# An early 64-byte store of zeros to every partition's rows of the output, in a streaming multiply-add

## The chip, the cores and the metric

The kernel runs on one core of one Trainium2 chip. The metric is the device time of one execution in microseconds (us), and the medians below are over repeated runs. Every profile shows the clock at 1.0.

## The reference, cut to what matters

```python
B, S, D = 1024, 16, 512          # x, y: bfloat16 (B, S, D); gamma: bfloat16 (D)
def reference(x, y, gamma):
    return x + gamma * y
```

Two inputs of 16.8 MB are read and one output of 16.8 MB is written, and there is little arithmetic.

## The kernel before

The 16384 rows of 512 elements are spread over 128 partitions, 128 rows (128 KB) each. They are handled in four pieces of 32 rows, so a piece is 32 KB a partition and 4 MB in all. The x loads go through the SyncE queue and the y loads through the ScalarE queue. The stores are issued behind all the loads of their queue.

```python
    nc.gpsimd.dma_start(out=gamma_row[:], in_=gamma.unsqueeze(0))
    nc.vector.memset(ones_row[:], 1.0)
    gamma_ps = psum_pool.tile([P, D], mybir.dt.float32)
    nc.tensor.matmul(gamma_ps[:], ones_row[:], gamma_row[:], start=True, stop=True)
    nc.vector.tensor_copy(out=gamma_sb[:], in_=gamma_ps[:])
    io_pool = ctx.enter_context(tc.tile_pool(name="io", bufs=SLOTS))     # SLOTS = 6
    # ... cut ...
    for c in range(n_pieces):                                            # PIECE = 32, four pieces
        r = slice(c * PIECE, (c + 1) * PIECE)
        # ... cut: xt, yt from io_pool ...
        nc.sync.dma_start(out=xt[:], in_=xv[:, r, :])
        nc.scalar.dma_start(out=yt[:], in_=yv[:, r, :])
        # ... cut: yt = yt * gamma_sb, then yt = xt + yt, both on VectorE ...
    for c in range(n_pieces):
        r = slice(c * PIECE, (c + 1) * PIECE)
        eng = nc.sync if c % 2 == 0 else nc.scalar
        eng.dma_start(out=ov[:, r, :], in_=ys[c][:])
```

## Time and profile before

| What | Before |
|---|---|
| time, median of 3 runs | 123.46 us (123.09 to 123.53) |
| span in the profile | 121.5 us |
| bytes moved | 50.33 MB, mean 414 GB/s |
| VectorE busy | 70.4 us (58%) |
| one multiply or one add of a piece | 8.7 us |

Lines of the page of the kernel before. They are the busy time of an engine, the two DMA rows in 40 slices of the span (busy share in tenths, then GB/s), the packet count, the DMA queues with packets, MB and share of the 16 engines' time, and the chain of work that ended last.

```profile
span 121.5 us, 80 instructions
PE 0.6 (0%) x1; PEld 0.1 (0%) x1; DVE 70.4 (58%) x10; POOL 0.8 (1%) x5
...
DMA  5899999999999999999999999989898989898992
GB/s 173 378 486 389 475 399 464 399 464 421 442 432 432 410 453 410 453 399 464 410 453 410 453 410 453 345 345 518 356 507 356 507 356 507 367 496 389 475 410 108
DMA packets 1760, 50.33 MB, mean 414 GB/s; under 512 B 224, under 2 KB 224, under 8 KB 224
...
q10 hardware_dynamic: 864, 25.17, 48.7%
q1 hardware_dynamic: 864, 25.17, 48.6%
q0 software_dynamic: 32, 0.00, 0.0%
...
DMA yt<-in_y_dram 53%; DVE yt L58 14%; DVE yt L64 14%; ACTq L57 0%
```

The DMA row is at 8 or 9 nearly everywhere while VectorE is busy little more than half the time, so the 16 DMA engines set the time. The Trainium skill (HBM Reference, Specifications (TRN2)) says that a core streaming alone measures about 425 GB/s, bounded by its 16 DMA engines. This trace agrees, with 414 GB/s over the whole span, start and end included. The chain names VectorE for 29% of the span (two lines of 14.3%), but meanwhile the DMA engines are busy with other transfers, so this share is no limit.

The trace also holds a record of every DMA packet (queue, start, duration, size). One packet here is one partition's 32 KB. Undisturbed it takes 1.213 us, and each engine has 96 of them: 96 x 1.213 = 116.4 us. From the first packet (1.76 us) to the last completion (119.95 us) are 118.2 us, so little is lost. There are two losses that all engines share. The first x packets take about 1.8 us. The y packets that start at 77.6 us take 1.79 to 2.13 us, which loses 0.75 us an engine. The second loss, two packets before the first result packet, is called **the stall** below. A view by windows shows it without the records (columns: window, its length, busy time of each engine, clock, DMA busy share, GB/s). The kernel before:

```profile
core 0: us, PE busy (x) PEld busy (x) DVE busy (x) POOL busy (x), PEclk, DMA share, GB/s
75.20:77.60 2.40, 0.00 (x0) 0.00 (x0) 2.40 (x1) 0.00 (x0) 1.00 1.01 437
77.60:79.54 1.94, 0.00 (x0) 0.00 (x0) 1.42 (x1) 0.00 (x0) 1.00 1.01 270
79.54:83.20 3.66, 0.00 (x0) 0.00 (x0) 0.35 (x1) 0.00 (x0) 1.00 1.02 439
```

In the third line the DMA share is still 1.01 but the rate is 270 GB/s instead of 437. A DMA engine counts as busy while a packet is on it, moving or not. (A packet is put into the window where it starts, so windows have to be cut at packet starts for such a reading.)

### The profile page before, as it was taken

To read this page: it belongs to the slowest core of one execution; us is meant where nothing else is said; L and a number is where in the kernel's file an instruction comes from. 1 tells how busy PE (TensorE), PEld (TensorE's weight loads), DVE (VectorE), ACT (ScalarE), POOL (GpSimd) and SP (SyncE) were. 2 spreads that over 40 slices of the span, in tenths; PEclk is the share of its full clock that TensorE was granted. 3 is DMA by queue.
4 is the path that set the end of the run, shared out by engine and by line. 5 is a ranking of instruction groups with operands and counts; after the bars stand their busy time and mean duration, and the time that the engine had idled before them with its cause. 6 is when DMAs were issued, how large, how long until landed. Compare 5 with 4: busy or idle time off the path is not lost.

```text
span 121.5 us, 80 instructions
## 1 busy us (share of the span) xinstructions
PE 0.6 (0%) x1; PEld 0.1 (0%) x1; DVE 70.4 (58%) x10; POOL 0.8 (1%) x5
## 2 busy tenths in 40 slices
PE   0001000000000000000000000000000000000000
PEld 0000000000000000000000000000000000000000
DVE  0002000499999399999679999907999990000000
POOL 2000000000000000000000000000000000000000
DMA  5899999999999999999999999989898989898992
GB/s 173 378 486 389 475 399 464 399 464 421 442 432 432 410 453 410 453 399 464 410 453 410 453 410 453 345 345 518 356 507 356 507 356 507 367 496 389 475 410 108
DMA packets 1760, 50.33 MB, mean 414 GB/s; under 512 B 224, under 2 KB 224, under 8 KB 224
## 3 DMA queue, kind: packets, MB, share of 16 engines
q10 hardware_dynamic: 864, 25.17, 48.7%
q1 hardware_dynamic: 864, 25.17, 48.6%
q0 software_dynamic: 32, 0.00, 0.0%
HBM read 33.56 MB, written 16.78 MB: 414 GB/s over the span
## 4 chain that ended last, share of the span: by engine, by line
DMA 53%; DVE 29%; ACTq 0%; issue 0%
DMA yt<-in_y_dram 53%; DVE yt L58 14%; DVE yt L64 14%; ACTq L57 0%
## 5 line engine op out<-in xcount | busy, mean ns | idle before, releaser
L58 DVE TENSOR_TENSOR yt<-yt,gamma_sb 128x16384 bf16<-128x16384 bf16 x4 | 34.8, 8692 | 18.9 <-DMA yt<-in_y_dram 18.9
L64 DVE TENSOR_TENSOR yt<-xt,yt 128x16384 bf16<-128x16384 bf16 x4 | 34.8, 8692 | 0.1
L47 DVE CAST gamma_sb<-gamma_ps 128x512 bf16<-128x512 f32 x1 | 0.7, 692 | 10.1 <-PE gamma_ps L46 10.1
L44 DVE MEMSET ones_row<- 1x128 bf16 x1 | 0.2, 165 | 0.8 <-PEq L85 0.8
L46 PE MATMUL gamma_ps<-gamma_row,ones_row 1*128 1x512 bf16 x1 | 0.6, 579 | 10.4 <-DMA gamma_row<-in_gamma_dram 10.4
L43 POOL DMA_DIRECT2D gamma_row<-in_gamma_dram x1 | 0.6, 607 | 0.8 <-POOLq L85 0.8
L46 PEld LDWEIGHTS <-ones_row 1*128 1x128 bf16 x1 | 0.1, 98 | 1.0 <-DVE ones_row L44 1.0
L85 POOL MEMSET const-bfloat16-1.0<- 128x1 bf16 x1 | 0.1, 97 | 0.0
L85 POOL MEMSET const-float32-0.0<- 128x1 f32 x1 | 0.1, 93 | 0.2 <-issue 0.2
L85 POOL MEMSET const-float32-1.0<- 128x1 f32 x1 | 0.1, 94 | 0.0
L85 POOL MEMSET const-uint8-127<- 128x1 uint8 x1 | 0.1, 94 | 0.0
## 6 DMA issues: line engine op xcount, KB each, us to landing
yt<-in_y_dram ACTq DMA_DIRECT2D x4, 4096.0 KB, 32.1
xt<-in_x_dram SPq DMA_DIRECT2D x4, 4096.0 KB, 40.5
out_dram<-yt SPq DMA_DIRECT2D x2, 4096.0 KB, 49.0
out_dram<-yt ACTq DMA_DIRECT2D x2, 4096.0 KB, 31.1
gamma_row<-in_gamma_dram POOLq DMA_DIRECT2D x1, 1.0 KB, 9.2
```

Of the source, the lines that this page charges most:

```text
L43: nc.gpsimd.dma_start(out=gamma_row[:], in_=gamma.unsqueeze(0))
L44: nc.vector.memset(ones_row[:], 1.0)
L46: nc.tensor.matmul(gamma_ps[:], ones_row[:], gamma_row[:], start=True, stop=True)
L47: nc.vector.tensor_copy(out=gamma_sb[:], in_=gamma_ps[:])
L58: nc.vector.tensor_tensor(out=yt[:], in0=yt[:], in1=gamma_sb[:, None, :].to_broadcast([P, PIECE, D]), op=mybir.AluOpType.mult,)
L64: nc.vector.tensor_tensor(out=yt[:], in0=xt[:], in1=yt[:], op=mybir.AluOpType.add)
L85: nc = _bacc.Bacc("TRN2", target_bir_lowering=False, num_devices=1)
```

## The change

Its intent is to store something to the output early, so that whatever the first write to it may cost is met before the first store of results. 64 bytes of zeros go to the start of every partition's rows through the GpSimd queue. The first store of results writes the same bytes, so it has to come after it and overwrites it.

```diff
     nc.vector.tensor_copy(out=gamma_sb[:], in_=gamma_ps[:])
+    prime_sb = const_pool.tile([P, 32], dt)
+    nc.vector.memset(prime_sb[:], 0.0)
+    nc.gpsimd.dma_start(out=ov[:, 0, 0:32], in_=prime_sb[:])
     io_pool = ctx.enter_context(tc.tile_pool(name="io", bufs=SLOTS))
```

## The prediction

> **What bounds the kernel now.** The DMA engines. The page's slice rows show DMA nine tenths busy or more nearly throughout, and 414 GB/s over the 121.5 us span; VectorE is busy 58%, the other engines almost never. The chain of waits (53% DMA, 29% VectorE) says it less directly, as queued transfers hide its VectorE part. In the packet records of the trace each of the 16 engines moves 96 data packets of 32 KB, at 1.213 us each when undisturbed: 116.4 us. The first packet starts at 1.8 us and the last completion is at 119.9 us: 118.2 us, so only 1.8 us is lost. Two losses hit all engines together: the first x packets take 1.82 us (0.6 us lost), and the y packets that start at 77.6 us take 1.8 to 2.1 us (mean 1.96; 0.75 us lost). The second comes two packets before the first result packet: queues run first in, first out, so the first store, issued at 40.6 us, moves only after all of x has landed, at 80.8 us. The other stores start without such a loss.
>
> **What the change adds.** One VectorE memset of 128x32 (the 1x128 one took 0.17 us; VectorE idles until 22.8 us) and a small DMA through GpSimd: 128 pieces of 64 bytes, eight an engine, behind the gamma load, whose packets were seen at 7.2 us and completions at 9.6 us. Small packets of that queue take turns with the two big queues, two packets of 1.213 us between turns: the pieces should move from about 9 us, and if each takes its own turn the last lands at about 32 us. The first store then waits for this DMA too (same bytes), but it can't move before 79 us, so that wait is free. The Trainium skill (DMA: Bandwidth & Descriptors, Specifications) says that below 512 bytes the engine does a read-modify-write; no run here shows that yet. Gamma's 64-byte packets took 0.011 us each. I estimate 0.01 to 0.1 us a piece, 0.1 to 0.8 us an engine, all of it on the critical path.
>
> **What it may remove.** The 0.75 us loss, if it is a cost of the first write to the output (something set up once for these addresses, that lasts 70 us). The small store then meets it early: either it is hidden there, because 64 bytes hold up little, and 0.75 us is gained; or it blocks load packets just as long, and nothing is gained. If the loss comes of turning from loads to stores, it stays, and the small store adds one or more of its own. Loads, multiplies, adds and stores keep their order on every engine.
>
> **Prediction.** 123.46 - half of 0.75 + about 0.2 = 123.2 us, range 122.3 to 124.3. Faster by over 2% (under 121.0): 0.02, since 1.8 us is all that is lost anywhere. Within 2%: 0.95. Slower by over 2%: 0.03, if every piece stalls its engine by 0.75 us (8 x 0.75 = 6 us).
>
> **What would show it.** Packet records: y packets near 77 us at 1.21 us mean the first-write theory holds; still 1.9 us, that it falls. Long load packets at 9 to 32 us show a loss that only moved. The slice rows stay as they are; packets rise by 144 (128 pieces, 16 completions); the first result store shows no wait for the small store.
>
> **What would make it wrong.** Stalls at every piece; a GpSimd queue that holds up the engines; the small store landing after 79 us.

## The result, and the profile after

The changed kernel takes 123.45 us (median of 4 runs, 123.19 to 123.60) beside 123.41 us before (4 runs). The ratio is 1.0005, with a 95% interval of 0.998 to 1.003: the same. Here and below a ratio is the mean time of one kernel's runs over that of the other's in the same rounds, so not quite the ratio of the medians.

The page of the changed kernel, the lines that answer to those above, then the new store's lines among the groups of instructions (busy us, mean ns, idle before) and the DMA issues (KB each, us from issue to landing):

```profile
span 121.6 us, 83 instructions
PE 0.6 (0%) x1; PEld 0.1 (0%) x1; DVE 70.4 (58%) x11; POOL 1.4 (1%) x6
...
DMA  6898989999999989898989898999899999999991
GB/s 172 366 496 367 498 388 474 399 463 420 442 453 409 474 388 485 377 485 377 485 377 485 377 496 366 345 388 474 388 474 399 463 399 463 409 453 442 420 463 54
DMA packets 1792, 50.34 MB, mean 414 GB/s; under 512 B 240, under 2 KB 256, under 8 KB 256
...
q0 software_dynamic: 64, 0.01, 0.0%
...
L52 POOL DMA_DIRECT2D out_dram<-prime_sb x1 | 0.6, 559 | 0.0
...
out_dram<-prime_sb POOLq DMA_DIRECT2D x1, 8.0 KB, 13.3
```

What SyncE's DMA queue waited for in the changed kernel (us in total, times, longest). The line of the loads is L61 here, that of the result stores L75:

```profile
SPq L75 <- DVE yt L69: 37.0, 1, 37.0
...
SPq L75 <- DMA xt<-in_x_dram: 0.9, 1, 0.9
```

The windows around the stall, changed kernel:

```profile
75.10:77.49 2.39, 0.00 (x0) 0.00 (x0) 2.39 (x1) 0.00 (x0) 1.00 0.98 411
77.49:79.54 2.05, 0.00 (x0) 0.00 (x0) 1.45 (x1) 0.00 (x0) 1.00 1.03 272
79.54:83.30 3.76, 0.00 (x0) 0.00 (x0) 0.00 (x0) 0.00 (x0) 1.00 1.02 436
```

There are three things to see here.

1. The small store cost next to nothing. It is 32 packets more (q0 from 32 to 64): 16 of data and 16 completions. The packet records show the data as one packet of 512 bytes an engine, at 12.0 to 12.4 us, of 0.027 us each; its completions come at 14.4 to 14.8 us. No load packet between 9 and 32 us took more than 1.213 us. No result store shows a wait for it: the waits of SyncE's queue name the add and an x load only.
2. The stall is still there. It moves 272 GB/s at a share of 1.03, and the 16 y packets at 77.5 to 78.5 us take 2.03 us in the mean, against 1.96 before.
3. So a term of gain that did not come and a cost that is too small to see leave the time where it was.

What remains is why the stall did not care.

### The profile page after: what moved, and what is told of

The parts are those of the page before. It is cut to its first block, busy times and chain, and to the rows that moved or that the text cites. A ratio compares the mean times of both kernels' runs of the same rounds, so it can differ in the third digit from the quotient of the medians.

```text
span 121.6 us, 83 instructions
## 1 busy us (share of the span) xinstructions
PE 0.6 (0%) x1; PEld 0.1 (0%) x1; DVE 70.4 (58%) x11; POOL 1.4 (1%) x6
## 4 chain that ended last, share of the span: by engine, by line
DMA 54%; DVE 29%; ACTq 0%; issue 0%
DMA yt<-in_y_dram 54%; DVE yt L63 14%; DVE yt L69 14%; ACTq L62 0%
## 5 line engine op out<-in xcount | busy, mean ns | idle before, releaser
L52 POOL DMA_DIRECT2D out_dram<-prime_sb x1 | 0.6, 559 | 0.0
```

The costliest lines, as they stand in the source:

```text
L52: nc.gpsimd.dma_start(out=ov[:, 0, 0:32], in_=prime_sb[:])
```

## The experiments

The measure in all of them is the loss: the sum over data packets of duration minus undisturbed duration for that size (1.213 us for 32 KB, 0.611 us for 16 KB, 0.311 us for 8 KB), divided by 16 engines. Smaller packets are left out. It counts every data packet of these sizes that took longer, whatever the reason, so a load packet that is held up beside a small early packet is in it too. It was worked out from the packet records of one profile a kernel, by when the packets start:

```
us from span start      1-4    4-28   28-41   41-60   60-76   76-83   83-90  90-122  after 4 us
before                 0.60    0.00    0.02    0.10    0.06    0.77    0.00    0.00     0.95
before_again           0.58    0.00    0.00    0.05    0.05    0.73    0.00    0.00     0.83
after                  0.65    0.00    0.00    0.04    0.05    0.93    0.00    0.00     1.03
pieces16               0.52    0.02    0.28    0.26    0.00    0.15    0.00    0.00     0.73
turns                  0.42    0.02    1.26    0.00    0.00    0.00    0.01    0.10     1.39
mixed                  0.62    0.00    0.00    1.03    0.00    0.00    0.16    0.00     1.19
touch_4k               0.71    0.08    0.04    0.12    0.29    0.58    0.00    0.00     1.12
touch_rows             0.70    0.45    0.03    0.07    0.05    0.09    0.00    0.00     0.69
touch_other            0.65    0.46    0.03    0.07    0.05    0.30    0.00    0.00     0.91
sbuf_first             0.49    0.00    0.00    0.05    0.05    0.64    0.00    0.00     0.75
hbm_first              0.59    0.00    0.00    0.05    0.06    0.10    0.49    0.00     0.70
sbuf_early             0.73    0.97    0.05    0.07    0.05    0.03    0.00    0.00     1.17
aligned                0.53    0.01    0.00    0.04    0.09    0.59    0.00    0.00     0.73
uneven                 0.64    0.00    0.00    0.43    0.77    0.00    0.00    0.00     1.20
```

Two theories stood at the start. *First write*: the stall is met once, when bytes of the output are first written, and one 64-byte piece a partition was too little or in the wrong place to meet it. *Turning*: an engine loses time whenever it turns from loads to stores.

### before_again: does the stall repeat?

The kernel before, unchanged.

> The kernel before, unchanged, profiled a second time: how well the stall repeats. If it belongs to the first stores, 0.6 to 0.9 us a packet on all engines near 77 us again. If it is chance, or set by how the two queues happen to stand to each other (the run with 16-row pieces showed only 0.2 us), it is clearly different this time.

The loss was 0.73 us at the same place (0.77 in the first profile), and the time of the one run 123.30 us. The stall belongs to the kernel and is not chance.

### pieces16: the control for the next

```diff
-PIECE = 32
-SLOTS = 6
+PIECE = 16
+SLOTS = 12
```

> The kernel before in pieces of 16 rows (8 pieces, 12 slots), loads first as before: the control for the run with more turns. Both theories: one stall of about 0.75 us on every engine, just before the first result packets, near 77 us. First-write theory and turning theory do not differ here. Time within 1.5 us of the kernel before.

The time was 123.38 us beside 123.19 (ratio 1.0004, 0.9981 to 1.0027). The loss near 77 us was only 0.15 us. Another 0.54 us was spread thinly over 28 to 60 us, where the loads took 0.615 to 0.63 us a packet instead of 0.611. So both theories missed where it would fall, and no run explains it: 0.73 us is lost after the start here too, but not in one stretch.

### turns: three turns to stores instead of one

The loop is cut into functions for one load step and one store, and called in the order shown (16-row pieces, 12 slots).

```diff
+    for step in "L0 L1 L2 S0 S1 L3 L4 S2 S3 L5 L6 L7 S4 S5 S6 S7".split():
+        (load if step[0] == "L" else store)(int(step[1:]))
```

> Pieces of 16 rows, and both queues turn together from loads to stores three times (near 31, 60 and 99 us) and back twice (near 41 and 70 us). First-write theory (a cost met once when result bytes are first written): one stall of about 0.75 us, before the first stores near 29 us; later turns show packets of 1.21 us, unless each new piece of the output counts as new, which then shows at every store piece. Turning theory (the pipeline of an engine runs dry when its source changes): a stall of 0.6 to 0.8 us at each of the three turns to stores, and perhaps 0.6 us at each turn back, so 1.5 to 3 us longer than with one turn.

The first turn lost 1.26 us, the two later ones nothing measurable (0.00 from 41 to 83 us, 0.11 from then on). The turning theory falls: the loss is met once. The time, 124.59 us (ratio 1.0116), is longer for another reason as well. The last add ends at 115.9 us, so the last store comes late, and the engines have no packet for 0.8 us in the mean between the first packet and the last. That time is not used as evidence for either theory.

### mixed: load and store packets in alternation

```diff
     for c in range(n_pieces):
+        if c == 2:
+            nc.sync.dma_start(out=ov[:, 0:PIECE, :], in_=ys[0][:])
         r = slice(c * PIECE, (c + 1) * PIECE)
     # ... cut ...
-    for c in range(n_pieces):
+    for c in range(1, n_pieces):
```

> The first store is put between the second and the third x load, so that from about 41 us every engine takes a store packet and a y load packet in turn, 16 times. First-write theory: one stall of about 0.75 us near 39 us, then 1.21 us a packet. Turning theory: every change from a load packet to a store packet costs something, up to 0.75 us each, 8 changes an engine or more: up to 6 us lost between 39 and 61 us. The whole time is longer for another reason too, as x comes later and the last multiply with it; the packet records are what counts.

The loss is 1.03 us, all of it in y packets that start between 41.2 and 44.7 us; the alternation that follows until 60 us loses nothing. The time of the one run was 123.49 us. Turning costs nothing by itself, once more. The first-write theory expected one stall, and there was one.

### touch_rows, touch_other, touch_4k: more early pieces, and elsewhere

The change, with its small store widened. touch_rows puts 64 bytes into every row (1 KB) that the first result store writes:

```diff
-    nc.gpsimd.dma_start(out=ov[:, 0, 0:32], in_=prime_sb[:])
+    nc.gpsimd.dma_start(out=ov[:, 0:PIECE, 0:32], in_=prime_sb[:, None, :].to_broadcast([P, PIECE, 32]))
```

> The change with 64 bytes stored early to each of the 32 rows of every partition that the first result store writes (4096 pieces, 32 times as many, one in every KB). First-write theory with a unit smaller than 32 KB: the stall near 77 us is gone (packets of 1.21 us), as every KB was touched before. Turning theory: the stall stays at 0.75 to 0.9 us. Cost of the pieces: the 8 of the change took 0.027 us an engine in one packet, so 32 times that is 0.9 us an engine, and the time grows by about 0.9 us; if each piece costs a read-modify-write of 0.1 us, by 25 us.

touch_other does the same in rows that the last result store writes:

```diff
-    nc.gpsimd.dma_start(out=ov[:, 0, 0:32], in_=prime_sb[:])
+    nc.gpsimd.dma_start(out=ov[:, 3 * PIECE : 4 * PIECE, 0:32], in_=prime_sb[:, None, :].to_broadcast([P, PIECE, 32]))
```

> The early 64 bytes in every KB again (4096 pieces), but in the rows that the last result store writes and not the first. If the early pieces work by their addresses, the stall near 77 us is back at 0.7 to 0.9 us, and the time is about 0.7 us above the run that touched the first rows (124.0), so 124.6. If they work by anything else (the mere volume of early small stores, the engines put out of step with each other), the stall is as small as in that run, about 0.1 us, and the time is the same as there.

touch_4k does it in every fourth row of the first store's:

```diff
-    nc.gpsimd.dma_start(out=ov[:, 0, 0:32], in_=prime_sb[:])
+    nc.gpsimd.dma_start(out=ov[:, 0:PIECE:4, 0:32], in_=prime_sb[:, None, :].to_broadcast([P, PIECE // 4, 32]))
```

> 64 bytes early in every fourth KB of the rows of the first result store (1024 pieces). First-write theory with a unit of 4 KB or more (but under 32 KB, as one piece per partition did nothing): the stall near 77 us is gone, the pieces cost a quarter of the 1.3 us that 4096 took, and the time is 0.2 to 0.5 us below the kernel before. With a unit under 4 KB, or if addresses have nothing to do with it, the stall stays and the time is 0.3 us above.

touch_rows took 123.96 us beside 123.19 (ratio 1.0064, 1.0042 to 1.0085). Its stall near 77 us is 0.09 us, which alone looked like the first-write theory proved. Two things spoke against it. Its load packets had lost 0.45 us early, at 4 to 28 us, where the kernel before lost none. And touch_other, which wrote none of those addresses, lost the same 0.46 us early, had 0.30 us left of the stall, and the same time: 124.14 us beside 123.45 (ratio 1.0048, 1.0026 to 1.0069, which overlaps touch_rows). So writing to those addresses was not needed to bring most of the stall down; whether they account for the difference between 0.09 and 0.30 us, from one profile each, is open. touch_4k, with a quarter of the pieces, took 123.65 us beside 123.45 (ratio 1.0010, 0.9993 to 1.0028) and kept 0.58 us of the stall. It shows another 0.29 us at 60 to 76 us that I can't explain.

The pieces themselves took 0.83 us an engine in touch_rows (four packets of 4096 bytes, 0.209 us each in the mean) and 0.16 us in touch_4k (one packet). The x packet right behind each of these packets took 0.074 to 0.132 us longer than 1.213 us, and the one after that did not (at most 1.224 us). That is 0.34 us an engine in touch_rows and touch_other, and 0.07 us in touch_4k. So the early loss of these runs is mostly a cost of each early packet (another 0.07 to 0.08 us falls before 9 us, when no piece has moved yet), and not the stall in one stretch at an earlier place. In touch_rows the pieces cost about 1.2 us in all, more than the stall could have given back.

What brought the stall down in touch_rows and touch_other was not found. The text of touch_other names engines out of step as a rival, but the records do not bear it out: shortly before the stall up to 13 of the 16 engines work for the same queue at once in both runs, and only up to 11 in before_again, whose stall is whole.

### sbuf_first: is it the write to HBM, or SBUF as the source?

A small copy from SBUF to SBUF on each queue, between loads and stores.

```diff
+    side = const_pool.tile([P, 2, 4, D], dt)
     # ... cut: the loop of loads ...
+    nc.sync.dma_start(out=side[:, 0], in_=ys[0][:, 0:4, :])
+    nc.scalar.dma_start(out=side[:, 1], in_=ys[1][:, 0:4, :])
     for c in range(n_pieces):
         r = slice(c * PIECE, (c + 1) * PIECE)
```

> Between the loads and the stores each queue moves 512 KB from SBUF to SBUF, so that the turn from HBM as source to SBUF as source comes one transfer before the first write to HBM. First-write theory: no long packet at the turn to the SBUF copies; the stall comes with or just before the first store, 2.4 us later. If it belongs to the change of source: 0.7 us at the last loads, none at the stores.

Windows of sbuf_first (columns as above):

```profile
75.00:77.46 2.46, 0.00 (x0) 0.00 (x0) 2.46 (x1) 0.00 (x0) 1.00 0.99 426
77.46:79.30 1.84, 0.00 (x0) 0.00 (x0) 1.50 (x1) 0.00 (x0) 1.00 1.06 323
```

The first packet of a copy starts at 79.30 us and the first result packet at 82.93 us. The stall comes just before the copies and there is none just before the stores (0.00 us from 83 to 90 us). Nothing has been written to HBM when it comes, nor is anything to be written for 3.6 us. This speaks against first write, and for the source of the data. (The time, 125.48 us in one run, contains the copies.)

### hbm_first: writes to the output whose source is HBM

```diff
+    nc.sync.dma_start(out=ov[:, 96:104, :], in_=xv[:, 96:104, :])
+    nc.scalar.dma_start(out=ov[:, 104:112, :], in_=yv[:, 96:104, :])
     for c in range(n_pieces):
         r = slice(c * PIECE, (c + 1) * PIECE)
```

The rows that this fills are overwritten by the last store; the output was correct.

> Between the loads and the stores each queue copies 1 MB from HBM to HBM (into output rows that the last store overwrites). If the stall belongs to SBUF as the source of a large transfer, the turn to these copies is free of it (under 0.2 us) and the stall of 0.5 to 0.9 us comes about 5 us later, at the stores. If it belongs to the end of the loads or to any write to HBM, it comes at the last loads, near 77 us, as before.

Windows of hbm_first; its copies start at 78.7 us, its stores at 85.30 us:

```profile
75.00:77.50 2.50, 0.00 (x0) 0.00 (x0) 2.50 (x1) 0.00 (x0) 1.00 0.97 419
77.50:80.00 2.50, 0.00 (x0) 0.00 (x0) 1.52 (x1) 0.00 (x0) 1.00 1.03 439
...
82.50:85.30 2.80, 0.00 (x0) 0.00 (x0) 2.80 (x1) 0.00 (x0) 1.00 1.00 345
```

The first writes to the output, out of HBM, pass at full rate (439 GB/s where the kernel before had 270). The stall comes at the end of the copies, just before the first packets out of SBUF. That it now falls on the copies' own packets shows that it is not something about loads into SBUF. First write falls in its plain form. (These rows are not those of the first result store, so a cost for each address would be left; the next run takes that away too.)

### sbuf_early: the same source, early, and no write to HBM

```diff
+    side = const_pool.tile([P, 2, 4, D], dt)
+    zero = const_pool.tile([P, 1, D], dt)
+    nc.vector.memset(zero[:], 0.0)
     # ... cut, then in the loop, ahead of the loads of c ...
+        if c == 1:
+            nc.sync.dma_start(out=side[:, 0], in_=zero[:].to_broadcast([P, 4, D]))
+            nc.scalar.dma_start(out=side[:, 1], in_=zero[:].to_broadcast([P, 4, D]))
```

> Each queue moves 512 KB of zeros from SBUF to SBUF between its first and its second load (near 21 us); nothing is written to HBM early. If the stall is met once, at the first larger transfer out of SBUF whatever its target, load packets lose 0.5 to 1 us near 19 to 24 us and under 0.3 us near 77 us. If it needs writes to HBM, nothing near 21 us and 0.7 us at 77 us.

Windows of sbuf_early, first around its copies (they start at 22.67 us), then around the place of the old stall:

```profile
16.80:19.30 2.50, 0.00 (x0) 0.00 (x0) 0.00 (x0) 0.00 (x0) 1.00 0.97 419
19.30:20.74 1.44, 0.00 (x0) 0.00 (x0) 0.00 (x0) 0.00 (x0) 1.00 0.95 364
20.74:22.67 1.93, 0.00 (x0) 0.00 (x0) 0.00 (x0) 0.00 (x0) 1.00 1.02 272
75.00:77.40 2.40, 0.00 (x0) 0.00 (x0) 2.40 (x1) 0.00 (x0) 1.00 1.02 437
77.40:79.80 2.40, 0.00 (x0) 0.00 (x0) 2.40 (x1) 0.00 (x0) 1.00 1.01 437
79.80:82.20 2.40, 0.00 (x0) 0.00 (x0) 2.40 (x1) 0.00 (x0) 1.00 1.02 437
```

This shows what calls it up. The stall stands before the SBUF copies, with its old signature (272 GB/s at a share of 1.02), and near 77 us, before the first write of the whole kernel to HBM, nothing is left (0.03 us). It can be moved, but here moving it gained nothing: 0.97 us was lost early (0.90 us of it before the copies start) instead of 0.77 late. The time, 126.32 us in one run, is 3.0 us above before, and the copies' packets took 3.04 us an engine.

### aligned and uneven: a try for a better kernel, and a misreading

In pieces16 both queues come to their end of loads at the same packet and the loss there was small, while in the kernel before the y queue is two packets behind. "aligned" loads the last piece in two halves, x and y of a half sharing one slot, so that the queues stay level with 32-row pieces elsewhere:

```diff
-    for c in range(n_pieces):
-        r = slice(c * PIECE, (c + 1) * PIECE)
-        xt = io_pool.tile([P, PIECE, D], dt, tag="io")
-        yt = io_pool.tile([P, PIECE, D], dt, tag="io")
+    for c in range(n_pieces + 1):
+        if c < 3:  # ... cut: as before ...
+        else:
+            n = PIECE // 2
+            r = slice(3 * PIECE + (c - 3) * n, 3 * PIECE + (c - 2) * n)
+            both = io_pool.tile([P, PIECE, D], dt, tag="io")
+            xa, ya = both[:, :n, :], both[:, n:, :]
+        # ... cut: load xa and ya, multiply, add; the stores take (r, ya) ...
```

> The last piece is loaded in two halves (x and y of a half share a slot), so that both queues come to their end of loads at the same packet instead of two packets apart. If the stall needs one queue still loading while the other starts to store (the run with 16-row pieces had both turn together, and lost 0.2 us), it falls under 0.3 us and the time is 0.3 to 0.6 us below the kernel before. If that was chance, 0.7 us again near 77 us and the same time as before or 0.2 us more.

The time was 122.99 us beside 123.32 (ratio 0.9970, 0.9950 to 0.9991): 0.3% better, the best kernel. I first read its loss near 77 us as zero, and formed the theory that the next run tests. That was a mistake: I had counted only the 32 KB packets, and just there its packets are of 16 KB. Counted with them the loss is 0.59 us, as the windows of aligned also show:

```profile
74.00:77.40 3.40, 0.00 (x0) 0.00 (x0) 3.40 (x1) 0.00 (x0) 1.00 1.01 429
77.40:80.60 3.20, 0.00 (x0) 0.00 (x0) 3.20 (x2) 0.00 (x0) 1.00 0.99 348
```

So aligning does not remove the stall, and the 0.33 us must come from elsewhere. In the profiles 0.2 us of it lies after the last packet: the span ends 1.29 us after it in aligned and 1.50 us in before, while the last packet ends at 119.95 us in both. Why was not tried.

"uneven" is aligned with one load moved to the other queue, so that one queue stores while the other still loads:

```diff
-        nc.sync.dma_start(out=xa, in_=xv[:, r, :])
+        (nc.scalar if c == n_pieces else nc.sync).dma_start(out=xa, in_=xv[:, r, :])
```

> The aligned kernel with one load moved: x of the last half goes to the other queue, so that one queue starts to store near 70 us while the other still has 4 MB to load. Theory formed from the earlier runs: an engine loses 0.7 to 1.3 us once, when its first packets out of SBUF have packets from HBM still beside or behind them. Then load packets lose 0.7 to 1.3 us between 67 and 74 us, and the time is 0.6 to 1.3 us above the aligned kernel, so 123.6 to 124.3. Rival: the aligned kernel is free of the loss because of its 16-row halves or by chance; then this one has it no more than that, under 0.3 us, and the same time, about 123.0.

It took 123.37 us beside 123.28 (ratio 1.0009, 0.9995 to 1.0023), under the range that the theory gave. The loss was 0.77 us at 60 to 76 us, and another 0.43 us at 41 to 60 us that no theory has. As the text takes aligned to be free of the loss, which it is not, this run confirms nothing about alignment. It shows one more kernel with about 1 us lost after the start.

## Why the prediction was right or wrong

The time, 123.45 us, lies in the range of 122.3 to 124.3 us, and "within 2%" was right. A full gain of 0.75 us and none at all both lie in that range, so the time alone says nothing about the theory. Point by point:

- *What bounds the kernel* held: 414 GB/s before and after, DMA at 8 to 9 tenths. As only 1.8 us of 118.2 us is lost anywhere, no early store could have gained 2%.
- *The 0.75 us that may be removed, taken at half* was wrong by its whole size: nothing was removed. The prediction named the sign by which its first-write theory would fall, y packets near 77 us still at 1.9 us. They were at 2.03 us. Its rival, the cost of turning, also fell (turns, mixed), and the small store added no stall of its own (0.00 us from 4 to 28 us). In place of both, sbuf_first, hbm_first and sbuf_early show a loss that is met once, ahead of the first large transfer out of SBUF on the two big queues, whether it is written to SBUF or to HBM.
- *Why 64 bytes a partition did not meet it* is open. Sorted by the size of the early transfer out of SBUF, the loss near 77 us is 0.93 us for 8 KB (the change), 0.58 us for 64 KB (touch_4k), 0.09 and 0.30 us for 256 KB (touch_rows, touch_other) and 0.03 us for 1 MB (sbuf_early). That looks like a matter of volume. But the first three sizes went through the GpSimd queue and the last through the SyncE and ScalarE queues, and the pieces differ too (128, 1024 and 4096 of 64 bytes, then 1024 of 1 KB), so volume, pieces and queue were not told apart. A small early store through the SyncE and ScalarE queues would have tested it; it was not run. Only sbuf_early shows the stall itself at the earlier place.
- *A bigger early store did not help* in any run. The loss after the start is 0.7 to 1.4 us in all 14 profiles, and the pieces or copies come on top. In touch_rows and touch_other, though, 0.34 us of it stands behind the early pieces, so there the stall shrank without coming back whole elsewhere; the pieces cost more than that.
- *The cost of the small store*, put at 0.2 us (0.1 to 0.8 us an engine), was too high: 0.027 us an engine. The Trainium skill (DMA: Bandwidth & Descriptors, Specifications) says that below 512 bytes the engine does a read-modify-write. No cost of one shows in the change: its eight pieces took 0.0034 us each, and the load packet behind them kept its 1.213 us. In the touch runs the load packet behind each packet of 64 pieces took 0.074 us longer or more; whether that is a read-modify-write, no run shows.
- *Each piece takes its own turn, landing at 32 us* was wrong: the eight pieces of an engine went as one packet at 12.0 us. The Trainium skill (DMA: Bandwidth & Descriptors, Queues, rings and completion order) says just this, that an engine takes turns between queues by whole packets of up to 64 descriptors. The trace agrees: 8 pieces in 512 bytes, and in touch_rows 64 pieces in each packet of 4096 bytes, four packets an engine. So the packet count rose by 32, not by 144.
- *The first result store does not wait for the small store* held, as the waits of its queue show.

So the forecast of the time was right by luck of small terms, not by its mechanism. The two errors (a gain of about 0.4 us that did not come, a cost of 0.2 us that was 0.03 us) left it 0.25 us low.

What stays open: what the engine sets up, or gives up, once when data first leaves SBUF. The packets that are lengthened lie in the last 2 to 4 us ahead of the first one out of SBUF (from 77.6 us to 80.8 us in the kernel before, from 41.2 us to 44.5 us in mixed), so something ahead of the data is at work; no run shows what. Whether it is time lost, or a lead of the early packets that is only paid back, could not be told apart. That the loss after the start was never under 0.69 us in any order of transfers may look like the second, but in touch_rows, which has the 0.69 us, half of it stands behind the early pieces. Nor is the spread-out loss of pieces16 explained.

## What to carry to other kernels

Read the DMA rate beside its busy share, in windows cut at packet starts: a share of 1.0 at 270 GB/s is a stall that neither the busy row nor the chain shows. Before warming something up early, find out which of its properties costs (its address, its direction, its source, its volume), by giving the suspected one alone, early and without the others; here an early transfer that wrote nothing to HBM moved the stall, and early writes at the wrong addresses took most of it away too (0.30 us left, 0.09 us at the right ones). And ask whether the cost disappears by being met early or is only paid at another time: in sbuf_early it was only moved (0.97 us early for 0.77 us late). Before a loss found early is called the moved one, look at which packets it stands on: in touch_rows it stood on the one packet behind each early piece.

## What the Trainium skill lacked or had wrong

- None of its pages on DMA and HBM has the loss met once at the first larger transfer out of SBUF: 0.5 to 1.3 us an engine in most runs, and moved to about 20 us by 1 MB of SBUF-to-SBUF copies (0.97 us there, 0.03 us at the old place). It would belong to DMA: Bandwidth & Descriptors.
- DMA: Bandwidth & Descriptors, Specifications, warns of transfers below 512 bytes (read-modify-write). In touch_4k a packet of 64 such pieces, stored to HBM, took 0.159 us: 26 GB/s an engine, beside 27 GB/s for 32 KB in 1.213 us. The load packet behind it took 0.074 us longer; with that counted it is about 18 GB/s. In touch_rows the first packet of each engine took 0.159 us too and the three later ones 0.225 us or slightly more; no run shows why.
- The same section gives about 1 us to the first byte for a DMA through GpSimd. Here the gamma load is issued at 1.22 us and its packets move at 7.2 us, behind the busy queues. Waiting for a turn may explain 2.4 us of it (two packets of 1.213 us): in pieces16, with packets of 0.611 us, they move at 6.0 us, 1.2 us sooner. The rest is not explained by any run.
